# Attention and mixture-of-experts kernel: matmuls on zeros placed in TensorE's plan, and a plan without its cold-clock term

## The chip, the cores and the metric

The kernel runs on one core of one Trainium2 chip. The metric is the device time of one execution in microseconds. A core has five engines with a queue each: PE (TensorE, matmuls and transposes into PSUM), ACT (ScalarE, the tanh and the exponentials), DVE (VectorE, copies and small arithmetic), POOL (GpSimd, casts, masks and the issue of the weight loads) and SP (which issues most loads and stores). An engine works through its own queue in order; an instruction that waits holds up all behind it on that engine. The TensorE clock can be throttled: the profile shows the share that was granted.

## What is computed

Two stages, the second on the output of the first. The first is attention with a soft cap on 8 batches of 12 heads, 448 tokens, head size 64. The second is a layer of four attention experts, of which each token uses two.

```python
# stage 1, per batch and head
scores = (q @ k.T) / 8
scores = cap * tanh(scores / cap)          # cap = 30
attn   = exp(scores - max); attn /= sum
x      = attn @ v                          # heads joined: 448 x 768 per batch
# stage 2, per batch, experts e = 0..3 of size 64
logits = x @ w_gate                        # two largest of four, softmax over them
q, k, v = x @ wq[e], x @ wk[e], x @ wv[e]
a      = softmax(q @ k.T / 8, causal)
out   += weight[e] * (a @ v @ wo[e])       # for the tokens that chose e
```

## The kernel before

**Tiling.** Two heads of a batch make a pair, so there are 48 pairs, six to a batch. The 448 keys of a head are 384 in three chunks of 128 and a tail of 64; the tails of both heads of a pair share one chunk (`ktz`, `vtz`). For each pair the kernel loads q, k, v and the tails (SP's queue, two pairs at a time, six pairs ahead), casts them to half precision on POOL (`a_cast`, `a_castv`: q, k, two key tails, v, two value tails), transposes q and k on PE (`a_tr`, into a tile `tps`, copied by DVE to `qt` and `kt`), multiplies scores (`fill`, into a tile `s`), takes the tanh of them (`tanh`, L516) and the exponential of a whole pair (`expo`, L522), multiplies by v (`a_pv_mm`, tile `pv`), divides (`a_pv_rc`, `a_pv_xk` on DVE) and transposes the result (`a_xt_tr`, tile `xtp`) into `xT`, which stage 2 reads. The last four pairs are worked in two passes over the queries, in this kernel and in the changed one.

**Scores in four parts.** A pair's scores come in four fills: the tail chunk (one matmul of 448 columns, L482) and three chunks (two matmuls each, L486). They go into two buffers of two PSUM banks, so fill i can start when the tanh of fill i-2 is done. On ACT the first tanh of a pair comes ahead of the exponential of the pair before: tanh 0 of pair p, exponential of p-1, tanh 1 to 3 of p. When ACT is through with tanh 1 and 2 it needs fill 3.

**Stage 2 in the gaps.** When the six pairs of a batch are done, `batch` adds the work of stage 2: projections `qps`, `kps` (`b_qk`) and `vps` (`b_v`), scores `sB` (`b_fill`) that share the two score buffers, their exponentials (L787) on ACT, `pvB`, `otp`, `wops` and the stores. The weights come by loads that POOL issues (`loads`, L1063), two or three per pair in the first pairs. Batch 0's scores stand in ACT's program within pairs 9 and 11.

**Banks.** All other products of PE (`tps`, `pv`, `xtp`, `qps`, `vps` and so on) take turns in four PSUM banks, the pool `aux`: `bank` gives the next of the four, and a tile's first matmul waits until the bank's last user has been read.

**What sets the order.** ACT's program (`prog`) is fixed beforehand. All else on PE is placed by a planner when the kernel is built (`Plan`). Each piece of work has a cost on PE and DVE, the pieces it depends on, a due time and the way it uses a bank (`aux`). The planner keeps its own clocks for PE, DVE and ACT. Ahead of each fill, `do_fill` lets it place the pieces that fit before the scores are due (`pump`, `step`): of those that can start within 0.3 us of the earliest, the one with the earliest due time. For casts and weights it assumes times: cast i is done at 5.0 * i + 1.0, a weight 26 us after its issue. PE costs are doubled for work that starts before `COLD` = 15 us of the planner's clock (`pe_time`). `slot(p)` runs once per pair in ACT's program: it issues loads, casts and weight loads, and adds the pair's pieces to the plan.

**The start.** Seven matmuls on a tile of zeros (`warm`, 512 columns each, tile `dummy`) are the first work of PE, while the first loads come in. Then pair 0 is cast, transposed and filled by hand, and from pair 1 on the planner goes on.

`gate_exp` puts the small exponential of a batch's gate (`eexp`) into ACT's queue as soon as the planner's clock says that the logits are there.

Of the kernel before, what the change touches and what calls it, by code (L numbers as in the profile page):

```python
# [10 lines left out]
f32 = mybir.dt.float32  # L11
# [6 lines left out]
class Plan:  # L18
# [3 lines left out]


    LAT = 0.2

    COLD = 15.0

    def pe_time(self, us, at):
        return us * (2.0 if at < self.COLD else 1.0)

    def __init__(self):
        self.pe = self.dve = self.act = 0.0
        self.done = {}

        self.aux = [0.0] * 4
        self.opened = set()
        self.work = []
# [13 lines left out]
    def emit(self, u):  # L51
        start = max(self.pe, self.ready(u))
        u["fn"]()
        self.pe = start + self.pe_time(u["pe"], start)
        end = self.pe + (self.LAT if u["aux"] != "open" and u["aux"] else 0.0)
        if u["dve"]:
            self.dve = max(self.dve, end) + u["dve"]
            end = self.dve + self.LAT
        if u["aux"] in ("open", "whole"):
            self.aux.pop(0)  # L60
        if u["aux"] == "open":
            self.opened.add(u["group"])
        self.done[u["key"]] = end
        if u["aux"] == "close":
            self.opened.remove(u["group"])
            self.done[u["group"]] = end
        if u["aux"] in ("close", "whole"):
            self.aux.append(end)

    def step(self, until, latest):  # L70


        at = {}
        for u in self.work:
            r = self.ready(u)
            if r is not None and max(r, self.pe) + self.pe_time(u["pe"], self.pe) <= latest:
                at[u["key"]] = max(r, self.pe)
        if not at:
            return False
        first = min(at.values())  # L80
        u = min(
            (u for u in self.work if at.get(u["key"], 1.0e9) <= first + 0.3),
            key=lambda u: u["due"],
        )
        if first > until:
            return False
        self.work.remove(u)
        self.emit(u)
        return True
# [156 lines left out]
def kernel(  # L246
# [13 lines left out]
    nc = tc.nc  # L260

    B, H, S, Dh = q.shape
# [31 lines left out]
    def bank(shape, dtype, name):  # L294
        return bank_pool[0].tile(shape, dtype, name=name, tag=bank_pool[1])
# [39 lines left out]
    warm = const.tile([128, 512], f16, name="warm")  # L335
# [39 lines left out]
    def evac(dst, src, act=False):  # L375
        (nc.scalar.copy if act else nc.vector.tensor_copy)(dst, src)  # L376
# [5 lines left out]
    def a_cast(p):  # L382
        if p >= NP:
            return
        eng = nc.vector if p < 2 else nc.gpsimd
        assert p < 8 or ("tr", p - 8) in plan.done
        assert p < 12 or ("pv", p - 12, 1) in plan.done
        qf, kf, vf, ktf, vtf = staged.pop(p)
        q16 = hd.tile([QP, QC, 2, Dh], f16, name=f"q16_{p}", tag="q16", bufs=8)
        k16 = hd.tile([128, KC, 2, Dh], f16, name=f"k16_{p}", tag="k16", bufs=8)  # L390
        eng.tensor_copy(q16, qf.rearrange("p h (c d) -> p c h d", c=QC))  # L391
        nc.gpsimd.tensor_copy(  # L392
            k16, kf.rearrange("p h (c d) -> p c h d", c=KC)
        )
        for g in range(2):
            r = slice(64 * g, 64 * (g + 1))
            eng.tensor_copy(ktz[p % 8][r, r], ktf[r, :])  # L397
        cast[p] = (q16, k16)
        vcast[p] = (vf, vtf)
        if p > 1:  # L400
            a_castv(p)
# [12 lines left out]
    def a_tr(p):  # L414
        q16, k16 = cast.pop(p)
        qps = bank([128, 1024], f16, f"tps_{p}")

        kps = qps[:, S : S + 512] if p else bank([128, 512], f16, "tpsk")
        for c in range(QC):
            nc.tensor.transpose(  # L420
                qps[:, c * QP : (c + 1) * QP],
                q16[:, c, :, :].rearrange("p h d -> p (h d)"),
                ident[0:QP, 0:QP],
            )
        nc.tensor.transpose(kps[:, 0:128], ktz[p % 8], ident)
        for c in range(KC):
            nc.tensor.transpose(  # L427
                kps[:, 128 * (c + 1) : 128 * (c + 2)],
                k16[:, c, :, :].rearrange("p h d -> p (h d)"),
                ident,  # L430
            )


        qt = hd.tile([128, S], f16, name=f"qt_{p}", tag="qt", bufs=8)
        kt = hd.tile([128, 512], f16, name=f"kt_{p}", tag="kt", bufs=8)
        m = qps[:, 0:S].rearrange("m (c p) -> m c p", c=QC)
        nc.vector.tensor_copy(  # L437
            qt[:, 0:KM].rearrange("m (n c t) -> m n c t", n=3, c=QC),
            m[:, :, 0:96].rearrange("m c (n t) -> m n c t", t=32),
        )  # L440
        nc.vector.tensor_copy(qt[:, KM:S].rearrange("m (c t) -> m c t", c=QC), m[:, :, 96:QP])
        evac(kt, kps, act=(p == 0))
        qkt[p] = (qt, kt)
# [453 lines left out]
            b_store(b, n)  # L897


    dummy = bank([128, 512], f32, "dummy")  # L900
    for _ in range(7):
        nc.tensor.matmul(dummy, warm[:, 0:128], warm, start=True, stop=True)

    plan = Plan()
    a_cast(0)
    a_tr(0)
    a_cast(1)
    for f in load(4):
        f(nc.sync)
# [110 lines left out]
    def do_fill():  # L1020
        nonlocal nfill
        o = reads[nfill]
        rel = ends[nfill - 2] + 0.15 if nfill >= 2 else 0.0
        cost = 0.36 if o[0] == "X" or o[2] or isinstance(o[1], tuple) else 0.19
        for d in fill_dep(o):
            plan.force(d)
        cost = plan.pe_time(cost, plan.pe)
        at = plan.act + sum(dur(x) for x in prog[pos : where[nfill]])
        rel = max(rel, *(plan.done[d] for d in fill_dep(o)))
        plan.pump(rel, max(rel + 0.05, at - cost - 0.25))  # L1030
        plan.pe = max(plan.pe, rel) + cost
        if o[0] == "T":
            fill(*o[1:])
        else:
            (l_fill if o[1] == B - 1 else b_fill)(*o[1:])
        plan.done[("f", nfill)] = plan.pe + plan.LAT
        nfill += 1
# [9 lines left out]

    def slot(p):

        if p % 2 == 0:  # L1050
            for i in ahead(p, LOAD, DEEP):
                if i % 2 == 0:
                    for f in load(i):
                        f(nc.sync)
        for i in ahead(p, CAST, DEEP + 2):
            a_cast(i)
            plan.done[("cast", i)] = max(
                5.0 * i + 1.0, plan.act + 4.0 + 3.5 * (i - p - CAST) * (p == DEEP + 2)
            )
        for _ in range(3 if p else 2):  # L1060
            if loads:
                w, dst, src = loads.pop(0)
                nc.gpsimd.dma_start(dst, src)  # L1063
                plan.done["w", w] = plan.act + 26.0
        if p in (4, 5):
            b_const(p - 4)
        for i in (1, 2) if p == 0 else ahead(p, TR, DEEP + 4, 4):
            plan.add(("tr", i), 0.43, 0.95, [("cast", i)], nom["S", i] - 3.0, a_tr, i)
        if 1 <= p < len(UNITS):
            u = UNITS[p - 1]  # L1070
            es = [("E", u)]
            due = nom["S", p + 1] + 2.0
            if isinstance(u, tuple):
                i = "AB".index(u[1])
                u = u[0]
                plan.parts(("pv", u, i), 2, 0.47, 0.55, es, due, a_pv, u, i)
                d = [("pv", u, i)]
                plan.add(("xt", u, "AB"[i]), 0.12, 0.27, d, due, a_xt_part, u, i)
            else:
                plan.parts(("pv", u, 0), 2, 0.47, 0.55, es, due, a_pv, u, 0)  # L1080
                d = [("pv", u, 0)]
                plan.parts(("pv", u, 1), 2, 0.47, 0.55, d, due, a_pv, u, 1)
                plan.add(("xt", u), 0.22, 0.35, [("pv", u, 1)], due, a_xt, u)
        if p >= HP and p % HP == 0 and p < NP:
            batch(p // HP - 1)
        if p == NP - 1:
            last_qk()
        if p == NP:
            last_vg()
# [497 lines left out]
    ngate = 0  # L1587

    def gate_exp(wait=False):

        nonlocal ngate
        d = plan.done.get(("v", ngate, 3) if ngate < B - 1 else ("lgA",))
        if d is not None and (wait or d <= plan.act):
            b_gexp(ngate, "" if ngate < B - 1 else "A")
            plan.act = max(plan.act, d) + 0.1
            plan.done[("G", ngate)] = plan.act + plan.LAT
            ngate += 1

    nread = 0
    for pos, o in enumerate(prog, 1):  # L1600
# [11 lines left out]
        start = max(plan.act, plan.done[("f", nread)])  # L1612
# [48 lines left out]
```

## Time and profile before

| | us |
|---|---|
| median of 5 runs | 327.48 |
| lowest and highest run | 325.42, 329.25 |
| the profiled execution | 329.25 |
| its span, first to last instruction | 327.5 |
| ACT busy in the span | 306.9 |
| PE busy in the span | 280.4 |
| DVE, POOL busy in the span | 216.8, 158.0 |
| mean granted TensorE clock | 0.968 |

The page divides the span into 40 slices of 8.2 us, and shows for each engine the busy share of a slice in tenths; PEclk is the granted clock in tenths of full speed. Lists of waits say which engine and line waited for which, with the total, the number and the longest. A timeline row has the start, the length, the engine, the line, the operation with its tiles, how often it came in a row, and in brackets the idle time ahead of it with what ended it ("issue": nothing that the profile shows). A matmul's end is modelled and includes its latency, so rows of matmuls overlap. The groups that matter here:

```profile
L516 ACT ACTIVATE y<-s 128x896 f16<-128x896 f32 (+1 forms) x176 | 138.8, 930 | 3.6 <-PE s L482 2.4
L522 ACT ACTIVATE p<-y 128x3136 f16<-128x3136 f16 x44 | 128.8, 2927 | 0.1
L787 ACT ACTIVATE pBs<-sB 128x960 f16<-128x960 f32 (+1 forms) x28 | 30.8, 1115 | 3.2 <-PE sB L768 3.2
```

Of each group: total and mean length, then the idle time of the engine just ahead of it and what ended most of it.

### The profile page before, as it was taken

What the parts mean: (1) busy time and instruction counts of PE and PEld (TensorE: products, weight loads), DVE (VectorE), ACT (ScalarE), POOL (GpSimd) and SP (SyncE); (2) the same over time, 40 slices, a digit from 0 to 9 for tenths busy, and PEclk for the clock granted to TensorE, in tenths of its full rate; (3) what the DMA queues carried; (4) which work ended last, traced back from release to release, by engine and by line L of the source; (5) the groups of instructions that cost most, each with busy time, mean ns of one, the idle gap of its engine ahead of it and who ended that gap; (6) DMA issues with size and microseconds to landing.
All of it is one profiled execution on the core that took longest, in us unless ns stands there. A gap on an engine that the chain in (4) does not pass through costs nothing.

```text
span 327.5 us, 8966 instructions
## 1 busy us (share of the span) xinstructions
PE 280.4 (86%) x3379; PEld 179.0 (55%) x3379; DVE 216.8 (66%) x760; ACT 306.9 (94%) x311; POOL 158.0 (48%) x480
## 2 busy tenths in 40 slices
PE   6687769787899879998899979997899878999992
PEld 2354445545555555655655655655555654557761
DVE  4264535376776776669876877668756975578572
ACT  3999899699999999999999999999999999999882
POOL 4639988672923479972932658062915200220200
PEclk9997779799999998999999999999999999999997
DMA  7699999990064998769063952679012102020027
GB/s 164 171 249 251 191 221 211 230 196 6 35 189 120 265 243 215 219 192 219 2 179 136 236 131 78 188 205 207 3 49 97 27 0 99 0 75 2 3 98 240
DMA packets 65403, 46.20 MB, mean 141 GB/s; under 512 B 26000, under 2 KB 61968, under 8 KB 65360
## 3 DMA queue, kind: packets, MB, share of 16 engines
q1 hardware_dynamic: 54000, 43.19, 51.5%
q0 software_dynamic: 10512, 1.58, 7.4%
q10 hardware_dynamic: 848, 0.87, 0.8%
q8 instruction: 26, 0.43, 0.6%
q14 instruction: 17, 0.14, 0.1%
HBM read 36.19 MB, written 11.01 MB: 144 GB/s over the span
## 4 chain that ended last, share of the span: by engine, by line
ACT 63%; PE 16%; DMA 7%; issue 6%; POOL 4%; DVE 1%; SPq 1%; POOLq 0%
ACT y L516 29%; ACT p L522 24%; ACT pBs L787 7%; DMA wvg<-in_moe_wv_dram 4%; PE vps L646 3%; PE wops L869 2%; PE pv L556 2%; DMA vtf<-in_v_dram 2%; DMA qf<-in_q_dram 1%; PE s L486 1%; PE pv L550 1%; PE sB L768 1%; PE qkA L1162 1%; ACT pB L522 1%; POOL wvg L1063 1%
## 5 line engine op out<-in xcount | busy, mean ns | idle before, releaser
L516 ACT ACTIVATE y<-s 128x896 f16<-128x896 f32 (+1 forms) x176 | 138.8, 930 | 3.6 <-PE s L482 2.4
L522 ACT ACTIVATE p<-y 128x3136 f16<-128x3136 f16 x44 | 128.8, 2927 | 0.1
L795 POOL TENSOR_SCALAR_AFFINE_SELECT pBs<-pBs 128x128 f16<-128x128 f16 (+1 forms) x112 | 28.3, 280 | 110.1 <-ACT pBs L787 109.0
L556 PE MATMUL pv<-v16s,p 128*128 128x65 f16 x1056 | 58.3, 199 | 0.0
L486 PE MATMUL s<-qt,kt 64*128 64x448 f16 x264 | 48.7, 377 | 10.4 <-ACT y L516 8.1
L556 PEld LDWEIGHTS <-p 128*128 128x128 f16 x1056 | 50.1, 101 | 4.1 <-issue 1.1
L550 PE MATMUL pv<-vtzs,p 128*128 128x130 f16 x176 | 40.8, 232 | 12.7 <-ACT p L522 11.5
L569 DVE TENSOR_TENSOR xk<-pv,rc 128x256 f16<-128x256 f32 x96 | 40.7, 424 | 3.3
L565 DVE RECIPROCAL rc<-pv 128x4 f32<-128x4 f32 x96 | 17.2, 180 | 36.2 <-PE pv L556 34.6
L376 DVE COPY ob<-wops 128x384 f32<-128x384 f32 (+1 forms) x53 | 29.2, 553 | 8.4 <-PE wops L869 8.2
L550 PEld LDWEIGHTS <-p 128*128 128x128 f16 x176 | 17.6, 100 | 29.7 <-ACT p L522 19.1
L787 ACT ACTIVATE pBs<-sB 128x960 f16<-128x960 f32 (+1 forms) x28 | 30.8, 1115 | 3.2 <-PE sB L768 3.2
L486 PEld LDWEIGHTS <-kt 64*128 64x128 f16 x264 | 16.1, 94 | 30.7 <-issue 23.3
L391 POOL CAST q<-qf 112x512 f16<-112x512 f32 x46 | 28.2, 614 | 6.5 <-DMA qf<-in_q_dram 4.6
L646 PE MATMUL vps<-wvg,xT 128*128 128x260 f16 (+1 forms) x192 | 30.8, 280 | 0.2 <-DMA wvg<-in_moe_wv_dram 0.2
L869 PE MATMUL wops<-wo,oT 128*128 128x384 f16 x128 | 30.2, 330 | 0.3 <-ACT oT L376 0.3
L405 POOL CAST v16s<-vf 128x384 f16<-128x384 f32 x48 | 24.5, 511 | 4.8 <-DMA vf<-in_v_dram 2.0
L392 POOL CAST k<-kf 128x384 f16<-128x384 f32 x48 | 24.5, 509 | 3.7 <-DMA kf<-in_k_dram 3.7
L376 DVE COPY xT<-xtp 128x448 f16<-128x448 f16 (+2 forms) x52 | 19.1, 368 | 10.2 <-PE xtp L591 8.8
L437 DVE COPY qt<-tps 128x384 f16<-128x384 f16 x48 | 16.8, 350 | 13.0 <-PE tps L427 12.4
L410 POOL CAST vtzs<-vtf 64x64 f16<-64x64 f32 x96 | 22.7, 236 | 4.1 <-DMA vtf<-in_v_dram 1.3
L397 POOL CAST ktzs<-ktf 64x64 f16<-64x64 f32 x92 | 21.6, 234 | 2.8
(178 smaller groups left out, 513.4 us busy)
## 6 DMA issues: line engine op xcount, KB each, us to landing
qf<-in_q_dram SPq DMA_DIRECT2D x22, 448.0 KB, 6.2
out_dram<-ob SPq DMA_DIRECT2D x23, 384.0 KB, 2.7
kf<-in_k_dram SPq DMA_DIRECT2D x22, 384.0 KB, 6.8
vf<-in_v_dram SPq DMA_DIRECT2D x22, 384.0 KB, 6.0
ktf<-in_k_dram SPq DMA_DIRECT2D x44, 32.0 KB, 5.8
vtf<-in_v_dram SPq DMA_DIRECT2D x44, 32.0 KB, 5.3
out_dram<-ob SPq DMA_DIRECT2D x7, 192.0 KB, 2.8
kf<-in_k_dram SPq DMA_DIRECT2D x4, 192.0 KB, 3.4
```

Of the source, the lines that this page charges most:

```text
L376: (nc.scalar.copy if act else nc.vector.tensor_copy)(dst, src)
L391: eng.tensor_copy(q16, qf.rearrange("p h (c d) -> p c h d", c=QC))
L486: nc.tensor.matmul(sc[:, g, 0:S], kt[r, 128 * i : 128 * (i + 1)], qt[r, :], start=True, stop=True,)
L516: nc.scalar.activation(dst, src, AF.Tanh, scale=isc / capf)
L522: nc.scalar.activation(pt[:, 0:n], y.pop(u)[:, 0:n], AF.Exp, scale=capf)
L550: nc.tensor.matmul(pv[:, n, :, :], prob(p, w, 0, 0), vtz[p % 12], start=(n == 0), stop=False, skip_group_check=True,)
L556: nc.tensor.matmul(pv[:, n, g, :], prob(p, w, j, g), v16[p % 12][:, g, j - 1, :], start=False, stop=(j == KC), skip_group_check=True,)
L569: nc.vector.tensor_tensor(xt[p][:, 2 * i : 2 * i + 2, :, :], pv[:, :, :, 0:Dh], rc.broadcast_to((128, 2, 2, Dh)), ALU.mult,)
L646: nc.tensor.matmul(ps, xT[b][:, j, w : w + 128], wvg[:, j, 0 : ps.shape[1]], start=(j == 0 and first), stop=(j == NDC - 1), skip_group_che ...
L787: nc.scalar.activation(pb[:, o0 : o0 + n], st[b].pop(("sc", r, g))[:, 0:n], AF.Exp, scale=isc)
L795: nc.gpsimd.affine_select(out=blk, in_=blk, compare_op=ALU.is_ge, fill=0.0, base=0, pattern=[[1, n]], channel_multiplier=-1,)
L869: nc.tensor.matmul(ps, st[b]["oT", r][:, w : w + 128], wo2[r][:, f * (D // 2) : (f + 1) * (D // 2)], start=(r == 0), stop=(r == 1),)
```

## The change

Three things are changed.

1. The planner's `COLD` and `pe_time` are removed: PE costs are no longer doubled in the planner's first 15 us.
2. The matmuls on zeros become a function, `keep_warm`. It takes one `aux` bank and runs one matmul of 512 columns on zeros. Nine of them stand at the start instead of seven; two more stand behind the transposes of pair 0. In `slot`, 14 pieces of one such matmul are added to the plan for each of pairs 0 to 2, 8 for pairs 3 to 6 and 4 for pairs 7 to 12, with a cost of 0.22 us and a due time later than all others; those of the pair before that found no place are dropped. A matmul on zeros is read by nobody.
3. `gate_exp` gets a test that no gate is left, so that it isn't called once too often.

The plan places 71 of the added pieces. With the other costs it also orders other work differently on PE in pairs 0 to 13 and in pairs 28 to 41, and the instructions of DVE that follow from it. On ACT one `eexp`, on POOL one small memset and on SP one store change places.

```diff
--- before.py
+++ after.py
@@ -22,12 +22,6 @@
 
 
     LAT = 0.2
-
-    COLD = 15.0
-
-    def pe_time(self, us, at):
-        return us * (2.0 if at < self.COLD else 1.0)
-
     def __init__(self):
         self.pe = self.dve = self.act = 0.0
         self.done = {}
@@ -51,7 +45,7 @@
     def emit(self, u):
         start = max(self.pe, self.ready(u))
         u["fn"]()
-        self.pe = start + self.pe_time(u["pe"], start)
+        self.pe = start + u["pe"]
         end = self.pe + (self.LAT if u["aux"] != "open" and u["aux"] else 0.0)
         if u["dve"]:
             self.dve = max(self.dve, end) + u["dve"]
@@ -73,7 +67,7 @@
         at = {}
         for u in self.work:
             r = self.ready(u)
-            if r is not None and max(r, self.pe) + self.pe_time(u["pe"], self.pe) <= latest:
+            if r is not None and max(r, self.pe) + u["pe"] <= latest:
                 at[u["key"]] = max(r, self.pe)
         if not at:
             return False
@@ -897,13 +891,18 @@
             b_store(b, n)
 
 
-    dummy = bank([128, 512], f32, "dummy")
-    for _ in range(7):
-        nc.tensor.matmul(dummy, warm[:, 0:128], warm, start=True, stop=True)
+    def keep_warm(n=1):
+
+        dummy = bank([128, 512], f32, "dummy")
+        for _ in range(n):
+            nc.tensor.matmul(dummy, warm[:, 0:128], warm, start=True, stop=True)
+
+    keep_warm(9)
 
     plan = Plan()
     a_cast(0)
     a_tr(0)
+    keep_warm(2)
     a_cast(1)
     for f in load(4):
         f(nc.sync)
@@ -1024,7 +1023,6 @@
         cost = 0.36 if o[0] == "X" or o[2] or isinstance(o[1], tuple) else 0.19
         for d in fill_dep(o):
             plan.force(d)
-        cost = plan.pe_time(cost, plan.pe)
         at = plan.act + sum(dur(x) for x in prog[pos : where[nfill]])
         rel = max(rel, *(plan.done[d] for d in fill_dep(o)))
         plan.pump(rel, max(rel + 0.05, at - cost - 0.25))
@@ -1047,6 +1045,9 @@
 
     def slot(p):
 
+        plan.work[:] = [u for u in plan.work if u["key"][0] != "warm"]
+        for i in range(14 if p < 3 else 8 if p < 7 else 4 if p < 13 else 0):
+            plan.add(("warm", p, i), 0.22, 0.0, [], 1.0e9, keep_warm)
         if p % 2 == 0:
             for i in ahead(p, LOAD, DEEP):
                 if i % 2 == 0:
@@ -1589,7 +1590,7 @@
     def gate_exp(wait=False):
 
         nonlocal ngate
-        d = plan.done.get(("v", ngate, 3) if ngate < B - 1 else ("lgA",))
+        d = plan.done.get(("v", ngate, 3) if ngate < B - 1 else ("lgA",)) if ngate < B else None
         if d is not None and (wait or d <= plan.act):
             b_gexp(ngate, "" if ngate < B - 1 else "A")
             plan.act = max(plan.act, d) + 0.1
```

## The prediction

> **What bounds the kernel now.** I read the page first, then the waits of ACT, then ACT's timeline around them, then PE's busy time on a grid of 3.41 us with the clock beside it, then PE and POOL where PE stood.
>
> ```profile
> span 327.5 us, 8966 instructions
> PE 280.4 (86%) x3379; PEld 179.0 (55%) x3379; DVE 216.8 (66%) x760; ACT 306.9 (94%) x311; POOL 158.0 (48%) x480
> ACT  3999899699999999999999999999999999999882
> PEclk9997779799999998999999999999999999999997
> ```
>
> ACT (the tanh L516 and the exponentials L522, L787) is the bound: from slice 8 to slice 36 it never rests. What a change to PE can win is the ACT idle time ahead of that, plus the start and the tail. The few low digits of ACT stand where PEclk is low. ACT's waits over the span:
>
> ```profile
> ACT pBs L787 <- PE sB L768: 3.2, 1, 3.2
> ACT y L516 <- PE s L482: 2.4, 3, 1.2
> ACT y L516 <- PE s L486: 1.1, 2, 0.7
> ```
>
> Their places, from ACT's timeline:
>
> ```profile
> 34.56 0.54 ACT L516 ACTIVATE y<-s 128x448 f16<-128x448 f32 x1 [1.15 <-PE s L482]
> ...
> 45.64 1.35 ACT L516 ACTIVATE y<-s 128x896 f16<-128x896 f32 x2 [0.65 <-PE s L486]
> ...
> 51.72 1.35 ACT L516 ACTIVATE y<-s 128x896 f16<-128x896 f32 x2 [0.41 <-PE s L486]
> ...
> 66.25 1.02 ACT L787 ACTIVATE pBs<-sB 128x1024 f16<-128x1024 f32 x1 [3.24 <-PE sB L768]
> ```
>
> I call them A (1.15, pair 5's first scores), B (0.65, pair 6's last), C (0.41, pair 7's last) and D (3.24). The first scores at 7.61 (0.65) and one wait at 125.26 (0.64) are the rest. A to D are 5.45 us, 1.7% of the span: the most that the middle can give.
>
> PE in stretches of 3.41 us, laid so that the edges fall on the clock's changes (columns: stretch, length, PE busy, granted clock, DMA):
>
> ```profile
> 2.62:6.03 3.41, 2.47 (x13) 1.00 1.14 222
> ...
> 16.27:19.68 3.41, 3.41 (x41) 1.00 0.74 190
> ...
> 23.09:26.51 3.42, 1.54 (x24) 1.00 1.13 251
> 26.51:29.92 3.41, 3.33 (x30) 0.51 1.41 248
> ...
> 46.98:50.40 3.42, 2.33 (x28) 0.99 1.47 238
> 50.40:53.81 3.41, 3.24 (x41) 1.00 1.40 210
> ...
> 57.22:60.64 3.42, 1.48 (x10) 1.00 1.19 244
> 60.64:64.05 3.41, 3.41 (x29) 0.51 1.18 211
> ```
>
> A stretch with 1.5 us of work is followed by one at half clock; 2.3 us is enough to keep it, and a nearly full stretch brings it back. Four stretches are at half (26.5, 33.3, 43.6, 60.6). The row's 1.00 at the start is not to be trusted: two 448-column matmuls take 0.56 us at 14.78 and 0.36 at 19.98, so PE is at half until the full stretch that ends at 19.7.
>
> Why was PE idle? Ahead of D, at 60.07, it waited for weights:
>
> ```profile
> 60.07 0.54 PE L730 MATMUL qps<-xT,wq 128*128 128x448 f16 x2 [1.94 <-issue]
> ```
>
> The profile names no releaser; the second half of this wq was issued at 41.14, and the slowest wq landing took 18.8 us, which gives 59.94. Ahead of A, B and C the transposes of a pair (tps) waited for POOL's casts: pair 6's key tail was cast by 33.49, pair 8's by 43.57, pair 9's by 49.39.
>
> **The change, part by part.** *Dummies.* PE gets 150 rows, 75 matmuls of 512 columns with their weight loads: 2 more ahead of the first transposes, 2 behind them, 71 placed by the plan, the longest runs 7, 8, 8 and 7 behind the xT transposes of pairs 1 to 4. A dummy is 0.43 at half clock (spacing of the 7 old ones) and, by half, 0.215 at full: 16 us of PE time. Beside ACT they cost nothing while PE is done before the scores are due.
>
> At the start: 9 dummies from 1.25 end at 5.1; the query cast ends at 5.31, so they hide behind its DMA. The 2 behind the transposes (0.86) end by 7.0, and the scores wait for kt until 6.97. Cost 0 (bounds -0.2 if the clock comes back by then, +0.1 if not). The stretch 2.62 to 6.03 becomes nearly full, so I expect full clock from some 6 to 9 us on instead of 19.7. ACT never waited between 7.61 and 33.4, so this alone pays nothing.
>
> In the runs of 8, each dummy takes one of the four aux banks. The third or fourth waits until DVE has copied xT out of its bank. Behind the run of pair 2's xT: transposes of pair 5 end 28.8 (POOL ends 28.46), two score pairs and xT to 29.65, the fourth dummy starts about 30.5 behind DVE's 1.35 us of copies, the run ends 31.5. The exponentials of pair 3 are ready at 31.0. Then two pv groups (0.5) and the last score pair of pair 4 (0.4) end at 32.4; ACT wants them at 32.55. So 0, with 0.15 to spare; bounds 0 to 0.3 for each of four runs. Semaphore waits of a dummy on PE itself have no row; they name a matmul four banks back, 0.85 us earlier, so I take 0. Behind a run of three at pair 5's xT only 13 dummies are left (2.8 us of PE time), singly or in threes, where ACT had no wait: 0, at most 0.5.
>
> *The plan without COLD.* This moves real work. Pair 6's transposes now come behind pair 5's first scores, so A's cause goes (-1.15); pair 8's come behind pair 6's last scores, so B's goes (-0.65). But POOL's casts and the loads on SP's queue keep their order, hence their times, and are the next bound: pair 7's tail cast ends 38.53, which gives pair 6's first scores at 39.25 against 39.15 wanted (0.1 lost). Pair 9's cast ends 49.39, and its transposes still stand ahead of pair 7's last scores: 49.39 + 0.35 + two pv groups 0.5 + 0.4 = 50.65. In the trace that tanh starts at 51.72. So at C ACT is 1.07 ahead, whatever A and B gave; the 0.51 of vps, that stood there and waited for its weights, moved behind.
>
> *D.* The first two qps of the second weight half go from just ahead of sB to behind sB, scores, vps, xT and pair 11's transposes, some 2.2 us of PE work later. PE gets there at 59.95, when the weights land. From C to the second sB PE has 11.4 us of work by its rows (matmul pairs 0.38, pv group 0.25, vps 0.11 each, tps 0.51), from 50.2 to 61.6; ACT needs 11.3, from 50.65 to 61.95. So D goes: -3.24.
>
> What comes in its stead: between the end of its work at 47.1 and 49.39 PE waits 2.1 us for pair 9's casts, in the stretch 46.98 to 50.40; only 1.3 us of it is work. That is a half-clock stretch from 50.4: up to 1.7 us of PE time, with 0.35 of slack before D. Bounds 0 (an edge of the grid splits the idle time) and 1.6; I take 0.8, since an edge can fall anywhere in another execution. No dummy stands at this wait.
>
> The eexp of batch 0 comes two and a half tanh and one exponential earlier on ACT (4.9 us of its work). The logits' copy should be done when the second pBs ends (0, at most 0.3). On POOL the 0.15 us memset of one vall goes behind a pair's casts, and on SP one out store goes behind the seven loads of a two-pair block: the memset's reader (pvB) and the store's are far off, 0. PE's order is different again for pairs 28 to 41, where ACT never waited; 0, between -0.2 and +0.6. The tail's order is the same. The new test in gate_exp adds no instruction.
>
> *A rule against the change.* The row: after 1.48 to 1.79 us of work in 3.41, half clock. The Trainium skill (TensorE: Matmul & The Clock Gate, "HAM oscillation") puts the danger at idle gaps above about 3.4 us. No gap of PE reaches that; the longest is 1.94. By the rule the dummies have nothing to hold after the start, and only the reordering counts. By the row, four half stretches cost about 1.7 us of PE time each. For the sum the two differ little: A, B and D go by the reordering, and without the clock's part B might keep 0.3, while D's successor would be 0. By the rule -4.0, by the row -3.5. I go with the row, as its four cases are here.
>
> **Sum**: -1.07 (to C) - 3.24 (D) + 0.8 = -3.5. Span 327.5 becomes 324.0. The profiled run took 329.25, 1.75 more than its span, and was the slowest of five; the median is 327.48, so the usual run already carries fewer of these waits. I count three quarters of the gain for it: 327.48 - 2.6 = 324.9.
>
> **The rivals.**
> (1) All of it and more: PE warm early, no half stretch at 50.4, and 125.26's wait gone too. -3.5 - 0.8 - 0.6 = -4.9, about 322.7. For: the grid is free. Against: POOL's casts don't get faster. Chance 0.2.
> (2) It does not hold the clock where it matters: idle time lies at waits for POOL and DMA that the plan doesn't know, the dummies stand elsewhere, a half stretch falls on 50.4 and another wait takes D's place; only the 1.07 stays, or less: 326.5 to 328. Chance 0.15.
> (3) Slower: the runs of 7 and 8 block PE ahead of the pv groups. They decide from the point at which a run ends more than 0.8 us behind the exponentials it hides under (ACT's two tanh after them last 1.7, pv and scores need 0.9). At full clock I have 0.55; at half clock a run of 8 takes 3.4 us and ends 1.7 later, and what follows takes 0.9 more, so ACT loses 0.55 + 1.7 + 0.9 - 0.8 = 2.3 at each of four runs: 9.4 - 3.5 = +5.9, about 333. For: four banks, DVE copies ahead. Against: PE should be warm by then, and the runs fill the thin stretches. Chance 0.12.
> My forecast: 0.53, own range 323.3 to 326.5.
>
> **How the numbers follow.** About 1% (3.3 us) is what a measurement of this kernel can tell from no change. Faster by over 1% is below 324.2: all of (1) and 0.16 of the forecast, 0.36. Slower by over 1% is above 330.8: most of (3), 0.11. Same: 0.53. The range reaches from (1)'s middle to (2)'s upper end: 322.4 to 328.0.
>
> **What would show it.** Right: 82 dummies; granted clock 1.0 in the stretches at 26.5, 33.3, 43.6; no wait at A and B; the tanh of C near 50.6 with a wait near 0.8; pair 9's transposes waiting for ktzs; no "issue" wait on qps at 60, the second pBs between 62 and 63.6. Wrong: dummies at 0.43 after 10 us, score matmuls directly behind a run with ACT waiting, POOL's casts at other times than before, a new wait behind 80 us.

## The result, and the profile after

| | before | changed |
|---|---|---|
| median, us | 326.51 (80 runs) | 325.04 (43 runs) |
| lowest, highest, us | 324.68, 330.69 | 323.21, 331.11 |
| ratio of the changed kernel to before | | 0.995 [0.9937, 0.9963] |
| the profiled execution, us | 329.25 | 324.92 |
| its span, us | 327.5 | 323.1 |
| mean granted clock in it | 0.968 | 0.988 |

The changed kernel is half a per cent faster: predicted 324.9, measured 325.04. The two profiled executions differ by 4.3 us, the medians by 1.47, since the execution profiled before was one of the longest of its 80. What the waits A to D are in a usual run of before, no profile shows. First the head of the page of the changed kernel and its row of granted clock.

```profile
span 323.1 us, 9113 instructions
PE 287.1 (89%) x3454; PEld 179.7 (56%) x3454; DVE 218.6 (68%) x760; ACT 306.6 (95%) x311; POOL 158.0 (49%) x480
ACT  3999998999999999999999999999999999999891
PEclk9999999999999979999999999999999999999997
```

PE has 6.7 us more work, ACT the same as before to 0.3 us. PEclk keeps its 9 for 14 slices, in which it had four 7s before: the clock is held. The low digits of ACT that stood at A and D (slices 5 and 8 of before) are gone, and an 8 stands in slice 7, at C. ACT's waits for scores in the changed kernel (line numbers are six lower than before: tanh L510, exponential L516, L781, scores L476 and L480):

```profile
ACT y L510 <- PE s L480: 1.9, 2, 1.2
ACT y L510 <- PE s L476: 1.1, 2, 0.6
```

The wait for `sB` (3.2) is gone from the list, and the rest is 3.0 instead of 3.5. The places, from ACT's timeline:

```profile
6.97 2.97 ACT L510 ACTIVATE y<-s 128x448 f16<-128x448 f32 x4 [0.46 <-PE s L476]
...
27.06 1.35 ACT L510 ACTIVATE y<-s 128x896 f16<-128x896 f32 x2 [0.72 <-PE s L480]
...
50.56 1.35 ACT L510 ACTIVATE y<-s 128x896 f16<-128x896 f32 x2 [1.15 <-PE s L480]
...
61.68 1.08 ACT L781 ACTIVATE pBs<-sB 128x1024 f16<-128x1024 f32 x1
```

A and B have gone. C stands at 50.56, 1.16 earlier than the 51.72 of before, with more wait. D has gone: the second pBs starts at 61.68 without brackets, 4.57 earlier. Those two steps are the whole difference of the spans: 1.16 up to C, 3.4 more up to D, 4.4 at the end. Two more things are new. The first tanh comes 0.64 earlier (6.97 against 7.61; 0.34 of that is an earlier landing of the first q load, issued at 0.80 in both: its cast on DVE starts at 4.46 against 4.80), and a wait of 0.72 stands at 27.06, in pair 3. Neither shows in the end, because ACT stands at C anyway. PE around these places:

```profile
23.30 0.23 PE L419 MATMUL tps<-ident,ktzs 128*128 128x128 f16 x1 [1.26 <-POOL ktzs L391]
...
24.35 1.67 PE L898 MATMUL dummy<-warm 128*128 128x512 f16 x7
...
26.34 0.38 PE L898 MATMUL dummy<-warm 128*128 128x512 f16 x1
26.65 0.36 PE L480 MATMUL s<-qt,kt 64*128 64x448 f16 x2
...
49.35 0.23 PE L419 MATMUL tps<-ident,ktzs 128*128 128x128 f16 x1 [0.56 <-POOL ktzs L391]
...
59.44 0.54 PE L724 MATMUL qps<-xT,wq 128*128 128x448 f16 x2
...
61.09 0.40 PE L762 MATMUL sB<-qe,ke 64*128 64x320 f16 x4
```

At 49.35 the transposes of pair 9 wait for POOL's cast; that is what holds C. POOL's own rows show that its queue had stood before these casts, behind the landing of a weight (`wvg`):

```profile
46.66 0.53 POOL L1064 DMA_DIRECT2D wo<-in_moe_wo_dram  x1 [1.07 <-DMA wvg<-in_moe_wv_dram]
...
48.77 0.52 POOL L391 CAST ktzs<-ktf 64x64 f16<-64x64 f32 x2
```

At 59.44 the `qps` start with no wait in brackets, and `sB` is ready at 61.5, before ACT asks. At 23.30 pair 4's transposes waited 1.26 for POOL, and a run of seven dummies and one single stood between them and the last scores of pair 3 at 26.65, for which ACT waited.

PE and the clock in stretches of 3.41 us, as in the prediction:

```profile
2.62:6.03 3.41, 3.41 (x17) 1.00 1.14 210
...
26.51:29.92 3.41, 3.22 (x38) 1.00 1.39 256
...
46.98:50.40 3.42, 1.87 (x27) 1.00 1.64 208
50.40:53.81 3.41, 3.41 (x35) 1.00 1.39 245
...
118.66:122.07 3.41, 3.41 (x29) 0.66 1.10 251
```

The half clock at 26.5 is gone, and the thin stretch before 50.4 was not followed by one. Apart from the last few us, the only half clock left is near 119 us, behind the last dummy (81.1). In this execution the edges of the clock lie 1.06 us earlier than those of the rows: the half clock runs from 117.60 to 121.01, so it is spread over two rows. Before had a half clock there too, from 122.1 to 125.5, a fifth that the prediction did not list.

What the profile can't say is which part of the change paid. Order and clock changed together.

### The profile page after: what moved, and what is told of

The parts are those of the page before. It is cut to its first block, busy times and chain, and to the rows that moved or that the text cites. A ratio compares the mean times of both kernels' runs of the same rounds, so it can differ in the third digit from the quotient of the medians.

```text
span 323.1 us, 9113 instructions
## 1 busy us (share of the span) xinstructions
PE 287.1 (89%) x3454; PEld 179.7 (56%) x3454; DVE 218.6 (68%) x760; ACT 306.6 (95%) x311; POOL 158.0 (49%) x480
## 4 chain that ended last, share of the span: by engine, by line
ACT 64%; PE 14%; DMA 8%; issue 6%; POOL 4%; DVE 2%; SPq 0%; POOLq 0%
ACT y L510 30%; ACT p L516 24%; ACT pBs L781 8%; DMA wvg<-in_moe_wv_dram 4%; DMA qf<-in_q_dram 2%; PE wops L863 2%; PE vps L640 2%; PE pv L550 2%; DMA vf<-in_v_dram 1%; PE pv L544 1%; PE s L480 1%; ACT pB L516 1%; PE qkA L1163 1%; POOL q L385 1%; PE dummy L898 1%
## 5 line engine op out<-in xcount | busy, mean ns | idle before, releaser
L510 ACT ACTIVATE y<-s 128x896 f16<-128x896 f32 (+1 forms) x176 | 139.7, 948 | 3.1 <-PE s L480 1.9
L516 ACT ACTIVATE p<-y 128x3136 f16<-128x3136 f16 x44 | 129.6, 2945 | 0.1
L550 PE MATMUL pv<-v16s,p 128*128 128x65 f16 x1056 | 55.1, 194 | 0.0
L480 PE MATMUL s<-qt,kt 64*128 64x448 f16 x264 | 46.5, 358 | 7.5 <-ACT y L510 5.1
L550 PEld LDWEIGHTS <-p 128*128 128x128 f16 x1056 | 47.2, 98 | 3.5 <-issue 0.4
L544 PE MATMUL pv<-vtzs,p 128*128 128x130 f16 x176 | 39.6, 225 | 7.8 <-ACT p L516 6.2
L544 PEld LDWEIGHTS <-p 128*128 128x128 f16 x176 | 17.2, 98 | 26.2 <-ACT p L516 15.6
L781 ACT ACTIVATE pBs<-sB 128x960 f16<-128x960 f32 (+1 forms) x28 | 31.4, 1138 | 0.0
L480 PEld LDWEIGHTS <-kt 64*128 64x128 f16 x264 | 16.0, 93 | 27.5 <-issue 20.1
L640 PE MATMUL vps<-wvg,xT 128*128 128x260 f16 (+1 forms) x192 | 29.9, 275 | 0.0
L898 PE MATMUL dummy<-warm 128*128 128x512 f16 x82 | 23.8, 406 | 1.3 <-DVE warm L330 1.3
```

What stands on the lines that cost most here:

```text
L480: nc.tensor.matmul(sc[:, g, 0:S], kt[r, 128 * i : 128 * (i + 1)], qt[r, :], start=True, stop=True,)
L510: nc.scalar.activation(dst, src, AF.Tanh, scale=isc / capf)
L516: nc.scalar.activation(pt[:, 0:n], y.pop(u)[:, 0:n], AF.Exp, scale=capf)
L544: nc.tensor.matmul(pv[:, n, :, :], prob(p, w, 0, 0), vtz[p % 12], start=(n == 0), stop=False, skip_group_check=True,)
L550: nc.tensor.matmul(pv[:, n, g, :], prob(p, w, j, g), v16[p % 12][:, g, j - 1, :], start=False, stop=(j == KC), skip_group_check=True,)
L640: nc.tensor.matmul(ps, xT[b][:, j, w : w + 128], wvg[:, j, 0 : ps.shape[1]], start=(j == 0 and first), stop=(j == NDC - 1), skip_group_che ...
```

## The experiments

The theory: the order pays, by POOL's and the loads' times, and the held clock pays nothing, since ACT covers PE. The rival: the held clock is what makes PE early. All kernels here compute the whole output; those without dummies leave out only matmuls on zeros that nobody reads. Ratios are to runs of the kernel before on the same chip (medians 326.57, 326.88 and 326.32 in the three groups of runs), with a 95% interval.

### The order without the dummies

The plan keeps its added pieces, so all other work is placed as in the changed kernel, but a piece emits nothing and takes no bank; the start is as before.

```diff
-    keep_warm(9)
+    keep_warm(7)
-    keep_warm(2)
-            plan.add(("warm", p, i), 0.22, 0.0, [], 1.0e9, keep_warm)
+            plan.add(("warm", p, i), 0.22, 0.0, [], 1.0e9, lambda: None)
```

> The changed kernel's order of all real work on every engine, with none of the 75 added matmuls on zeros (the plan counts them and emits nothing; seven at the start as before). Theory 1 (my prediction: the gain of A, B and D comes from the order that the plan takes without COLD, the held clock adds little): ratio to before 0.994 to 0.998, no wait of ACT at pair 5's first and pair 6's last scores, no 'issue' wait of qps near 60 us, the second pBs before 64 us, though stretches at half clock are there again. Theory 2 (the gain comes from the held clock): ratio 0.999 to 1.003, with the waits of before back where PE is at half clock.

Measured: 324.94 (324.07 to 325.96), 0.996 [0.9941, 0.9979]: all of the changed kernel's gain. Its row of granted clock, then PE's stretches in it:

```profile
PEclk9997779999999999999999999999999999999998
```

```profile
23.09:26.51 3.42, 1.53 (x26) 1.00 1.12 262
26.51:29.92 3.41, 3.26 (x34) 0.54 1.27 238
...
36.75:40.16 3.41, 2.99 (x31) 0.54 1.45 201
...
43.57:46.98 3.41, 3.26 (x40) 0.55 1.45 246
```

Three stretches are at half clock (the edges lie 0.25 us later than those of the rows, hence the 0.54), and the mean over the runs is 0.965 (before, in the same group, 0.960; changed kernel 0.992). ACT lost only small waits:

```profile
16.17 0.92 ACT L510 ACTIVATE y<-s 128x896 f16<-128x896 f32 x1 [0.48 <-PE s L480]
40.03 0.54 ACT L510 ACTIVATE y<-s 128x448 f16<-128x448 f32 x1 [0.36 <-PE s L476]
46.02 0.55 ACT L510 ACTIVATE y<-s 128x448 f16<-128x448 f32 x1 [0.32 <-PE s L476]
```

All three stand in or just behind stretches at half clock, so a slow PE does make ACT wait: 1.16 us here. The first tanh, too, is 0.72 later (7.69; 0.40 of it is the landing of the first q load). The changed kernel saves this, and loses 0.72 in pair 3 and 1.15 at C, behind POOL: the second pBs starts at 61.86 here and at 61.68 there. ACT has no wait at C here, as it comes there later and POOL did not stand ahead of the casts, which end 0.5 us earlier (the tail's rows start at 48.24 instead of 48.77):

```profile
48.24 0.53 POOL L391 CAST ktzs<-ktf 64x64 f16<-64x64 f32 x2
```

That the two sums come out so close in these two executions is chance. The theory's first half is shown by the medians, 324.94 and 325.04. Of its second half the result holds and the reason only in part: ACT does not cover PE everywhere, but what a full clock saves it is lost again behind POOL.

### The dummies without the order

The planner keeps `COLD`; nine and two dummies stand at the start, and runs as long as the plan's are put by hand behind the xT transposes of pairs 1 to 5: 44 matmuls on zeros in all, of the changed kernel's 82.

```diff
         a_xt_out(p)
+        keep_warm({1: 7, 2: 8, 3: 8, 4: 7, 5: 3}.get(p, 0))
...
+    keep_warm(9)
...
     a_tr(0)
+    keep_warm(2)
```

> The order of before for all real work, with 46 matmuls on zeros in the places of the changed kernel's long runs: nine and two at the start, then 7, 8, 8, 7 and 3 behind the xT transposes of pairs 1 to 5. Theory 1 (order): ratio to before 0.998 to 1.002; the wait of pair 5's first scores stays (0.8 to 1.2 us), as do the 'issue' wait of qps near 60 us and 2 to 3.5 us ahead of the second pBs. Theory 2 (held clock): ratio 0.993 to 0.997 and no stretch at half clock before 60 us. A rival that makes both slower (runs block PE): over 1.003.

Measured: 326.35 (324.80 to 329.15), 1.0004 [0.9975, 1.0032]: nothing that these runs can tell. The mean clock over the runs is 0.976. ACT's timeline, in the longest of the 12 executions:

```profile
35.12 0.54 ACT L516 ACTIVATE y<-s 128x448 f16<-128x448 f32 x1 [0.99 <-PE s L482]
...
62.54 0.97 ACT L788 ACTIVATE pBs<-sB 128x960 f16<-128x960 f32 x1 [1.25 <-PE sB L769]
...
67.11 1.02 ACT L788 ACTIVATE pBs<-sB 128x1024 f16<-128x1024 f32 x1 [2.78 <-PE sB L769]
```

A keeps 0.99 of its 1.15 although PE ran at full clock from 20 to 60 us, and D keeps 2.78 of its 3.24, with a wait of 1.25 at the first pBs that before did not have. B and C fell to 0.23 and 0.22. Ahead of D, PE stands longer than before (1.94), after 40 us of full clock. The profile names no releaser; I take it to be the weights again, as at this place in a later trace, where it names `wq`:

```profile
60.92 0.90 PE L731 MATMUL qps<-xT,wq 128*128 128x448 f16 x2 [2.84 <-issue]
```

### Each piece doubled

```diff
-            plan.add(("warm", p, i), 0.22, 0.0, [], 1.0e9, keep_warm)
+            plan.add(("warm", p, i), 0.22, 0.0, [], 1.0e9, keep_warm, 2)
```

The plan still counts 0.22 us for a piece that now has two matmuls.

> The changed kernel with two matmuls on zeros for each that the plan places, so that the long runs are 14, 16, 16 and 14 (3.0 to 3.4 us at full clock, 1.7 more than before). The plan's order of real work is the same. If the runs cost nothing until they end 0.8 us behind the exponential over them, as I reckoned (0.55 for the single run of 8), then doubled runs are late by 1 to 1.5 us at each of three or four places: 3 to 5 us more than the changed kernel, ratio to before 1.004 to 1.012, with waits of ACT behind each run. If PE's slack there is larger than I thought: within 0.3% of the changed kernel (0.993 to 0.998).

Measured: 328.97 (328.33 to 329.60), 1.0083 [1.0059, 1.0106], with a clock of 0.99. This is what rival (3) described, at full clock: PE's timeline and ACT's.

```profile
25.38 3.19 PE L898 MATMUL dummy<-warm 128*128 128x512 f16 x14
```

```profile
16.05 1.74 ACT L510 ACTIVATE y<-s 128x896 f16<-128x896 f32 x2 [0.96 <-PE s L480]
...
29.81 1.35 ACT L510 ACTIVATE y<-s 128x896 f16<-128x896 f32 x2 [1.09 <-PE s L480]
36.18 1.35 ACT L510 ACTIVATE y<-s 128x896 f16<-128x896 f32 x2 [0.69 <-PE s L480]
42.54 1.35 ACT L510 ACTIVATE y<-s 128x896 f16<-128x896 f32 x2 [0.69 <-PE s L480]
48.99 1.35 ACT L510 ACTIVATE y<-s 128x896 f16<-128x896 f32 x2 [0.78 <-PE s L480]
```

The scores of pair 3, at 29.81, come behind a run of 3.19 us where the changed kernel's took 1.67. Five such waits of 0.7 to 1.1 are 4.2 us in all; the second pBs starts at 66.10 instead of 61.68, and the median is 3.9 above the changed kernel's. There the runs end in time but for the 0.72 of pair 3; with 1.5 us more in each, ACT waits, though PE is at full clock from 20 to 116 us.

### The planner's COLD alone, taken from the kernel before

```diff
-    COLD = 15.0
+    COLD = 0.0
```

`gate_exp` gets the changed kernel's test. With no dummies in the plan some of PE's instructions stand differently from the changed kernel.

> The kernel before with COLD = 0 in the planner and nothing else (with the test in gate_exp that this order needs): no matmuls on zeros beyond the seven at the start, and none in the plan. If the gain is that of the removed term alone: ratio to before 0.994 to 0.998, as the changed kernel's order had without its dummies. If the places that the planned dummies take on the planner's clock are what shapes the good order: 0.998 to 1.002.

Measured: 324.62 (324.15 to 326.19), 0.993 [0.990, 0.996], at a clock of 0.964. ACT's waits in the middle are 0.48 at 16.19 and 0.58 at 40.07. One constant of the planner gives what the whole change gives; the intervals overlap.

### The planner's assumed times

POOL's key tails of pairs 6 to 9 end 2.5 to 3.4 us later than the plan assumes (pair 6's by 33.49 against 31, pair 9's by 49.39 against 46), and weights come later than its 26 us, which it counts from its own clock in the slot (POOL issued the second half of the `wq` ahead of D at 41.14, and the `qps` waited until 60.07; 8 us more was tried). The first kernel sets the casts right in the changed kernel:

```diff
-                5.0 * i + 1.0, plan.act + 4.0 + 3.5 * (i - p - CAST) * (p == DEEP + 2)
+                5.0 * i + (3.5 if 4 <= i < 10 else 1.0), plan.act + 4.0 + 3.5 * (i - p - CAST) * (p == DEEP + 2)
```

> The changed kernel with the planner's time for casts 4 to 9 put 2.5 us later (5.0 i + 3.5 in place of 5.0 i + 1.0), nearer to where POOL's casts end in the profile; the plan then puts the transposes of these pairs later, and the matmuls on zeros spread out. If the remaining waits (0.72 behind pair 4's transposes, 1.15 behind pair 9's) come from casts that the plan takes to be done too early, both go: ACT's waits between 7 and 70 us under 0.6 in sum, ratio to before 0.989 to 0.993. If they only move (late transposes make the next pair's first scores late, or the clock falls): 0.994 to 0.998.

Measured: 326.56 (324.03 to 329.05), 1.001 [0.9984, 1.0037]. A miss: the gain is gone. The 0.72 at 27.06 went as meant, but the plan, told that the casts are late, put `vps` ahead of pair 7's last scores, and its weights were not there; a wait of 0.79 at 57.74 came too. PE, then ACT:

```profile
50.43 0.51 PE L640 MATMUL vps<-wvg,xT 128*128 128x260 f16 x3 [2.77 <-DMA wvg<-in_moe_wv_dram]
50.87 0.36 PE L480 MATMUL s<-qt,kt 64*128 64x448 f16 x2
```

```profile
51.28 1.35 ACT L510 ACTIVATE y<-s 128x896 f16<-128x896 f32 x2 [2.71 <-PE s L480]
```

One wrong time was hidden by the other. So the weights next, in the kernel before, which keeps `COLD` (with the changed test in `gate_exp`):

```diff
-                plan.done["w", w] = plan.act + 26.0
+                plan.done["w", w] = plan.act + 34.0
```

> The kernel before, COLD kept, with the planner's time from a weight load's issue to its landing put at 34 us in place of 26. PE's order changes in pairs 7 to 12 alone: vps goes behind pair 7's last scores (place C) and the qps of the second weight half go behind sB, scores, vps and pair 11's transposes (place D); A and B stay as they were. My reading: D is the largest part of the gain, so ratio to before 0.995 to 0.998, no 'issue' wait of qps, less than 0.6 us of waiting ahead of the second pBs, with the waits at pair 5's first and pair 6's last scores still there. Rival (A and B carry it, and D was large only in the one profiled run): 0.999 to 1.001.

Measured: 326.24 (324.32 to 328.76), 0.9963 [0.993, 0.9996]. C and D are gone in the profile (the second pBs starts at 62.08 without wait), A stays with 1.24. B, expected to stay, is not there; a wait of 0.36 stands at 40.71 instead. The ratio makes the gain 0.37%, 1.2 us (the medians differ by 0.64), from the end of waits that were 3.65 us in the one execution profiled before, which points to a smaller D in a usual run. Then both times together, without and with `COLD` = 0:

> The kernel before, COLD kept, with weights at 34 us and casts 4 to 9 taken 2.5 us later (5.0 i + 3.5): transposes of pairs 6 to 9 go behind the scores they held up, vps and qps behind theirs. No matmul on zeros is added. Theory (all of A to D are orders in which PE meets a wait that the plan does not know): ACT waits under 1 us in sum between 8 and 70 us, ratio to before 0.990 to 0.995, and not slower than the changed kernel. Rival (each wait removed brings up another, as with the casts alone): 0.996 to 1.001.

> As the run before it, with COLD = 0 as well. If the term matters only by moving work past the waits, it adds nothing here: within 0.2% of that run (0.990 to 0.995 to before). If it does harm of its own at the start, where PE is at half clock until about 19 us and the plan takes it at full: ACT waits in the first 20 us, ratio 0.995 to 0.999.

Measured: with `COLD` kept 323.67 (323.00 to 325.97), 0.9891 [0.9838, 0.9944]; without it 323.50 (322.88 to 324.84), 0.9883 [0.9838, 0.9927]. Both lie below the changed kernel's 0.995 without one added dummy; the second's interval lies wholly below 0.9937, the first's reaches above it, as does that of the repeat below. With the times set later, `COLD` makes no difference that can be seen, which fits that its removal had won by moving work past these waits. The kernel with `COLD` kept has the lowest clock of all profiles here, 0.942, and from 7 to 113 us ACT waits for no score:

```profile
PEclk9587779997999899999999979998999999999997
```

```profile
7.13 2.97 ACT L516 ACTIVATE y<-s 128x448 f16<-128x448 f32 x4 [0.45 <-PE s L482]
113.80 0.54 ACT L516 ACTIVATE y<-s 128x448 f16<-128x448 f32 x1 [0.55 <-PE s L482]
```

The first row also shows the start of the changed kernel (6.97 with 0.46) reached with seven dummies.

### The dummies, once the times are right

The last group repeats the best kernel, adds the start's nine and two dummies to it, and sets both times right in the changed kernel with all its dummies.

> The kernel with COLD = 0, weights at 34 us and casts 4 to 9 taken 2.5 us later, run again beside the two below on one chip, as what they are compared with: 0.986 to 0.992 to before, mean granted clock 0.97 to 0.98.

> The same kernel and order with the start of the changed kernel: nine matmuls on zeros in place of seven, two more behind the first transposes. They should bring full clock from about 6 to 13 us on, not 19.7. If the start's clock is worth something: the one wait of ACT near 15.8 us (0.48) goes and the first tanh comes 0.2 earlier, 0.1 to 0.25% below the run beside it. If ACT covers it: within 0.1% of it.

> The changed kernel, matmuls on zeros and all, with weights at 34 us and casts 4 to 9 taken 2.5 us later: the same late times as the run beside it, with the clock held. Held clock worth nothing (my reading now): within 0.2% of the run beside it, mean clock over 0.985. Held clock worth something once the waits are gone: 0.2 to 0.6% below it. Dummies in the way: over 0.2% above it, with short waits of ACT behind a dummy.

| | us | ratio | mean clock |
|---|---|---|---|
| no added dummies, again | 323.48 (323.25 to 325.37) | 0.9917 [0.9885, 0.9949] | 0.981 |
| with those of the start | 324.26 (323.13 to 324.72) | 0.9926 [0.9899, 0.9954] | 0.966 |
| with all of them | 323.67 (322.59 to 325.58) | 0.992 [0.9889, 0.9952] | 0.992 |

The three can't be told apart. The repeat gives the same time as the first (323.50 and 323.48). The added start did not hold the clock: its profile shows half clock from 11.6 to 18.4 us, and the wait near 15.6 is still 0.48. ACT's timeline of the kernel with all dummies has two waits, the second of them at the old place of D:

```profile
54.64 1.39 ACT L510 ACTIVATE y<-s 128x896 f16<-128x896 f32 x2 [0.52 <-PE s L480]
61.63 1.02 ACT L781 ACTIVATE pBs<-sB 128x1024 f16<-128x1024 f32 x1 [1.24 <-PE sB L762]
```

In the main neither comes from the dummies. PE stood for a cast ahead of the first and for a weight ahead of the second (one dummy, some 0.3 us, stands in front of that `sB` too); in the repeat without dummies the same `qps` start at 58.17 and wait for nothing:

```profile
53.09 0.23 PE L419 MATMUL tps<-ident,ktzs 128*128 128x128 f16 x1 [0.56 <-POOL ktzs L391]
...
59.37 0.54 PE L724 MATMUL qps<-xT,wq 128*128 128x448 f16 x2 [1.19 <-DMA wq<-in_moe_wq_dram]
```

So there is the order with and without dummies (0.995, 0.996), the dummies without the order (1.0004), and the corrected times with and without dummies (0.992, 0.9917). The order pays; the dummies show no gain in either plan, within some 0.3% (1 us). That a held clock would be worth nothing in a plan that meets no late cast or load is not shown: with all dummies the last kernel still met both.

## Why the prediction was right

**The bound and the waits.** ACT's busy time did not move (306.9 and 306.6), and the gain is the two steps at C and D. Forecast span 324.0, measured 323.1: without the 0.8 for a half-clock stretch the sum gives 323.2.

**C.** Predicted at 50.65, by POOL's cast of pair 9, whatever A and B gave; measured at 50.56. The cast's time is less fixed than I took it to be: in the changed kernel and before, POOL stood 1.07 and 0.84 us for `wvg` ahead of it, in the order-only kernel it did not. The wait there was to be near 0.85 and is 1.15, since ACT came there earlier. This was the most useful step: the start's 0.64, A's 1.15 and B's 0.65 were all taken back at C, and so was the loss of 0.72 in pair 3.

**D.** Predicted gone, -3.24; it is. The second pBs was to start between 62 and 63.6 and starts at 61.68, because the next step took nothing.

**The half-clock stretch, +0.8.** The mis-sized term: it measured 0, the lower of its bounds. I had 1.3 us of work for the stretch from 46.98; it was 1.87, as four `qps` that stand ahead of pair 9's transposes start at 46.51, behind three dummies, and reach 0.45 us into it. Between this execution's own edges, 45.92 to 49.33, it is 1.88, some 0.6 of it those dummies, where I had written that none stands at this wait. The stretch behind it kept the clock. The margin was small, as the last section shows.

**The dummies, 0.** Right in the end, with one place mis-sized. I worked out the run of pair 2's xT (0.15 to spare, and it cost nothing) and let it stand for all four, with bounds 0 to 0.3. The run of pair 1's xT cost 0.72: it began late, because pair 4's transposes ahead of it waited 1.26 for POOL. C hides that price (with no late cast or with no dummies the scores would have come in time). The doubled pieces show what the same place costs when the runs are twice as long.

**Rule or row.** The Trainium skill (TensorE: Matmul & The Clock Gate, "HAM oscillation") speaks of idle gaps above about 3.4 us. Here the clock fell with no such gap: in the order-only kernel after a stretch with 1.53 us of work, its longest gap 1.89 us. So for the clock the row is the better guide. For the time they gave -3.5 (row) and -4.0 (rule), and the profiled spans differ by -4.4, but that doesn't decide between them, since the clock is not what the time hangs on: the kernels' mean clocks of 0.965, 0.992, 0.967 and 0.992 go with 324.94, 325.04, 323.67 and 323.67.

**Three quarters for the median.** Too much. Against the median of 80 the gain was 1.47 of the 4.33 between the profiled executions, a third. That 324.9 came out is luck: I forecast a gain of 2.6 where 1.47 was measured, and started from the five runs shown, whose median (327.48) lies 1.0 above that of 80. The mechanism does not rest on this luck; the number does. That D is smaller in usual runs is what the kernel with later weights points to; how the landing of the weights varies from run to run was not followed.

**The rivals.** (1), all and more, came half true: the clock was up early and the stretch at 50.4 stayed full, but the wait at 125.26 (0.64) is still there, at 120.75, in a half clock as before. (2) did not come. (3) came, with 2.5 us over before instead of 5.9, only with twice the dummies.

**Open.** A and B were not undone singly. The third change, the test in `gate_exp`, and the earlier `eexp` were not tried apart from the order. The start alone (a gain of up to 0.2 us in the first wait) is below what these runs can tell.

## What to carry to other kernels

Before giving a waiting engine something to keep it warm, ask whether it is the bound: here filler raised the mean clock from 0.965 to 0.992 at the same order and brought nothing that could be measured, because another engine covers most of PE's work and the waits that counted were for casts and loads. On an in-order engine with an order planned ahead, look in the trace for waits on things whose times the plan only assumes, and correct all of these together: one alone can bring the other out, as the casts did (1.001) until the weights were set too (0.992). And carry a saving to the next point where the engine has to wait anyway; what is won ahead of that point is lost there.

## What the hardware showed that I had not expected

- The clock changed in fixed steps. In each trace its falls lie a whole number of 3.413 us apart (26.57, 33.39, 43.63, 60.70 and 122.14 in the trace of before), with another offset in each execution. Laid on each execution's own edges, all falls between 20 and 310 us in the 13 traces follow a stretch with 0.69 to 2.08 us of PE work, and the stretches that kept the full clock had 1.88 or more. Between 1.88 and 2.08 both happened, so the 1.88 ahead of 49.33 was near the limit. A half clock ended only behind a stretch with 3.08 us or more. The busy times include modelled ends, so this is no exact limit.
- Matmuls on zeros count as work for it: with them no stretch from 23 to 117 us was at half clock, at the same order without them three were.
- The same first tanh came at 7.13 with seven dummies (wait 0.45), and at 7.60 and 7.69 in other kernels with the same seven (0.65). In the first of these a pair-0 score matmul of 448 columns took 0.36 us, in the order-only kernel 0.56. That the offset of an execution's clock edges decides this, more than two or four dummies do, is only argued; no run set the offset.
